# One ring tile of four PSUM banks in place of two two-bank tiles in the first phase of a ConvNeXt V2 block, with a new order of conv bursts and fewer channel-major quarters

## The chip, the cores and the metric

The kernel runs on one core of a Trainium2 chip. The time is the device time of one execution in microseconds (us), the median of several runs. All runs compared here were in the fast state. A ratio is the mean time of one kernel's fast runs over that of the other's from the same rounds, so it is not quite the ratio of the medians quoted beside it.

TensorE does the matmuls, ScalarE the activations out of PSUM, DVE (VectorE) the statistics and transposes, GpSimd (POOL in the profile) products in SBUF. The kernel uses PSUM as eight banks of 512 fp32 columns a partition: one, four and three in the pools below.

## The reference

```python
out = depthwise 3x3 convolution of x (1, 512, 512, 96)
h = layernorm(out, channels)
h = gelu(h @ w1)                                   # 96 -> 384
gx = sqrt(sum over all pixels of h*h + 1e-6)        # global, one value per channel
h = gamma * (h * gx / (mean(gx) + 1e-6)) + beta + h
return x + h @ w2                                   # 384 -> 96
```

The global sum splits the work into two phases. Phase 1 must see all pixels and make `sum h*h`. Phase 2 applies the result. The change touches phase 1 only.

## The kernel before

Phase 1 works on 128 blocks of four image rows (2048 pixels). In most of its *slots* TensorE makes the convolution of one block and the first MLP layer of an earlier block. The convolution is three *bursts* of 24 small matmuls on one accumulator of three banks (`psY`, one buffer), which ScalarE then copies out (`y_bf`, the *eviction*). The MLP is 12 banks of matmul output, each bank passed once through gelu by ScalarE.

The square sums come about in two ways. Output that stands channel-major (channels on partitions) goes through `bn_stats` on DVE, one instruction a bank. Output that stands pixel-major goes through *gram* matmuls on TensorE, three for each 128 pixels. A block has four quarters of 512 pixels, and `cm_quads` says how many are channel-major.

```python
def cm_quads(q):
    return 2 if is_res(q) else 3
...
psS = tile_pool(name="psS", bufs=1, PSUM)     # 1 bank: moments and gram sums, tile SG
psU = tile_pool(name="psU", bufs=2, PSUM)     # 2 x 2 banks: the MLP output
psY = tile_pool(name="psY", bufs=1, PSUM)     # 3 banks: the convolution
...
def pair(j):                                   # channels 128j.., two quarters, two banks
    U = psU.tile([128, 2, QW], f32, name="U")
    for t in range(2):
        cm_mm(U[:, t, :], j, t)
    act.activation(out=gsh[:, :, j, :], in_=U[:], func=Gelu_apprx_tanh)

def rest(n):                                   # two banks of the third quarter or of
    U = psU.tile([128, 2, QW], f32, name="U")  # pixel-major output
    ...
    act.activation(out=gms[b][:, c0:end], in_=Uf, func=Gelu_apprx_tanh)
...
# the order of a slot (cut)
conv(0); pair(0); conv(1); turn_x(s + 2)
pair(1); squares(0); gram_of_last(0)
pair(2); squares(1); gram_of_last(1)
rest(0); squares(2)
conv(2); evac()
rest(1); stats; rest(2); squares_rest()
```

`conv(n)` is burst n. Bursts 0 and 1 end in a drain of TensorE. No semaphore is written by hand: the recording layer (`tile.TileContext`) notes which instruction reads and writes which tile, and puts the waits in.

## Time and profile before

| | before |
|---|---|
| time | 1561.48 us (3 runs, 1561.41 to 1561.51) |
| conv evictions in 300 to 900 us | 80, so 7.5 us a slot |
| busy in that stretch: DVE, ScalarE, TensorE, GpSimd | 95, 93, 93, 89% |
| TensorE clock granted there | 1.00 |

The first fence is the busy table for 600 us in the middle of phase 1: length of the stretch, then for each engine busy us and instructions in brackets, then the granted TensorE clock, the share of the DMA engines, GB/s.

```profile
core 0: us, PE busy (x) PEld busy (x) DVE busy (x) ACT busy (x) POOL busy (x), PEclk, DMA share, GB/s
300.00:900.00 600.00, 557.30 (x9848) 269.83 (x9840) 572.30 (x963) 557.38 (x561) 537.04 (x403) 1.00 0.77 235
```

No engine is full. What sets the pace is seen in the timeline of one slot, first on TensorE (start, length, engine, operation, tiles, shapes, count, and in brackets the idle time before it and who ended it), then on ScalarE. All lines are of L32, a helper that records every operation, so the tile names tell them apart: Y is the convolution, U the MLP output, SG the statistics bank. The lengths of matmuls include their modelled ends and overlap; starts are what to compare.

```profile
531.53 0.88 PE L32 MATMUL Y<-xT,Wq 64*32 64x512 bf16 x24 [0.20 <-ACT y_bf L32]
532.53 0.60 PE L32 MATMUL U<-ynT,w1p 128*128 128x512 bf16 x2
533.06 0.86 PE L32 MATMUL Y<-xT,Wq 64*32 64x512 bf16 x24
534.05 0.60 PE L32 MATMUL U<-ynT,w1p 128*128 128x512 bf16 x2
...
538.94 0.87 PE L32 MATMUL Y<-xT,Wq 64*32 64x512 bf16 x24 [0.19 <-ACT y_bf L32]
```

```profile
533.22 1.02 ACT L32 ACTIVATE gsh<-U 128x1024 bf16<-128x1024 f32 x1
534.69 1.94 ACT L32 ACTIVATE gsh<-U 128x1024 bf16<-128x1024 f32 x2 [0.45 <-PE U L32]
536.51 1.03 ACT L32 ACTIVATE gm<-U 128x1024 bf16<-128x1024 f32 x1
537.42 1.47 ACT L32 ACTIVATE y_bf<-Y 128x1536 bf16<-128x1536 f32 x1
```

The first burst starts at 531.53 when the eviction is done. Pair, second burst and second pair follow; only then has ScalarE its second gelu (534.69, after 0.45 us of idleness). Three gelus and the eviction later, at 538.94, the next first burst can start. The waits of ScalarE in the 600 us say the same (total, times, longest):

```profile
ACT gsh L32 <- PE U L32: 42.4, 86, 1.5
```

### The profile page before, as it was taken

Reading aid. Unit: us, or ns where it says so; the run is one execution under the profiler, and the core shown is the slowest. Engines: PE = TensorE matmul, PEld = TensorE weight load, DVE = VectorE, ACT = ScalarE, POOL = GpSimd, SP = SyncE. Lnnn points to the kernel's source line nnn. Section 1 sums busy time; section 2 is a strip of 40 time slices with the busy share of each in tenths; the row PEclk is TensorE's granted clock in tenths of the full one; section 3 lists DMA queues with packets and bytes.
Section 4 is the critical chain, followed back from the end, with each engine's and each line's share of the span. In section 5 each row is a group of like instructions: output and inputs, shape, how many; then the busy total and the mean of one; then the engine's idle time right before and its main releaser. Section 6 shows DMA issues by size and latency. Waiting matters only on the chain. (4 is left out here: it accounts for less than half of the span.)

```text
span 1559.3 us, 54608 instructions
## 1 busy us (share of the span) xinstructions
PE 1438.9 (92%) x23119; PEld 819.7 (53%) x23119; DVE 1211.7 (78%) x2157; ACT 1436.7 (92%) x1306; POOL 1318.4 (85%) x933
## 2 busy tenths in 40 slices
PE   7889989999999999999999997789999999999998
PEld 3334444444444444444444443357777766676666
DVE  6749989999999999999999999955555555455555
ACT  3779989999999999999999999999999999899997
POOL 3459889989998998898899897459999999899997
PEclk8899999999999999999999999999999999999999
DMA  5568787777778778778868767879999999999996
GB/s 152 162 174 256 241 251 249 223 225 246 228 245 250 231 226 258 237 221 250 244 207 252 221 198 222 275 249 395 380 385 384 381 377 378 341 389 379 376 379 236
DMA packets 235467, 427.86 MB, mean 274 GB/s; under 512 B 34103, under 2 KB 148375, under 8 KB 235223
## 3 DMA queue, kind: packets, MB, share of 16 engines
q1 hardware_dynamic: 219972, 356.59, 70.4%
q0 software_dynamic: 13888, 67.64, 11.5%
q8 instruction: 181, 2.97, 0.8%
q14 instruction: 64, 0.52, 0.1%
q10 hardware_dynamic: 1362, 0.15, 0.1%
HBM read 272.78 MB, written 150.72 MB: 272 GB/s over the span
## 5 line engine op out<-in xcount | busy, mean ns | idle before, releaser
L32 PE MATMUL U<-ynT,w1p 128*128 128x512 bf16 x2292 | 664.4, 381 | 48.5 <-ACT gm L32 10.0
L32 ACT ACTIVATE gr<-U 128x1536 bf16<-128x1536 f32 (+1 forms) x384 | 519.1, 1456 | 13.1 <-PE U L32 11.3
L32 DVE BATCH_NORM_STATS2 bst<-gsh 128x6 f32<-128x512 bf16 x756 | 463.0, 674 | 21.7 <-ACT gsh L32 15.7
L32 DVE TENSOR_TENSOR o_sb<-O,xb 128x384 bf16<-128x384 f32 x512 | 277.9, 556 | 250.7 <-PE O L32 153.0
L32 POOL TENSOR_TENSOR yn<-y_bf,rbc 128x1536 bf16<-128x1536 bf16 x128 | 397.4, 3107 | 87.3 <-ACT rbc L32 31.0
L32 ACT ACTIVATE gsh<-U 128x1024 bf16<-128x1024 f32 x378 | 374.5, 1025 | 61.5 <-PE U L32 61.4
L278 POOL TENSOR_TENSOR xb<-xr,B2c 128x1536 f32<-128x1536 bf16 x126 | 394.8, 3135 | 33.9 <-DVE B2c L32 30.9
L32 ACT ACTIVATE gm<-U 128x1024 bf16<-128x1024 f32 x384 | 381.8, 1047 | 0.2
L32 PE MATMUL Y<-xT,Wq 64*32 64x511 bf16 (+1 forms) x8694 | 324.6, 391 | 32.9 <-ACT y_bf L32 25.8
L32 POOL TENSOR_TENSOR ysq<-y_bf 128x1536 bf16<-128x1536 bf16 x114 | 313.2, 2748 | 32.9 <-ACT y_bf L32 32.4
L32 PEld LDWEIGHTS <-w1p 128*128 128x128 bf16 x2292 | 181.6, 97 | 289.5 <-issue 203.3
L32 PEld LDWEIGHTS <-gr 128*128 128x128 bf16 x4584 | 236.8, 98 | 107.5 <-issue 23.4
L32 PE MATMUL O<-W2s,gr 128*128 128x96 bf16 x4584 | 257.2, 206 | 12.4 <-DVE o_sb L32 11.9
L32 DVE BATCH_NORM_STATS2 bst<-gm 128x6 f32<-128x512 bf16 x378 | 242.3, 679 | 29.7 <-ACT gm L32 29.7
L32 PEld LDWEIGHTS <-Wq 64*32 64x32 bf16 x9216 | 114.0, 91 | 212.5 <-issue 174.1
L32 ACT ACTIVATE y_bf<-Y 128x1536 bf16<-128x1536 f32 x121 | 177.5, 1467 | 16.2 <-PE Y L32 16.1
L32 DVE STREAM_TRANSPOSE xT<-xin 128x576 f32<-128x576 f32 (+1 forms) x256 | 180.4, 745 | 2.1 <-DMA xin<-in_x_dram 2.0
L32 PEld LDWEIGHTS <-gm 128*128 128x128 bf16 x1560 | 106.8, 98 | 66.3 <-issue 11.7
L32 PE MATMUL SG<-gm 128*128 128x128 bf16 x1560 | 126.1, 219 | 8.9 <-DVE SG L32 8.2
L32 PE MATMUL U<-w1p,ynT 128*128 128x384 bf16 (+2 forms) x780 | 126.5, 272 | 5.0 <-ACT gm L32 3.8
L250 POOL DMA_DIRECT2D xr<-in_x_dram x123 | 68.4, 556 | 35.9 <-POOL xb L278 35.9
L32 PEld LDWEIGHTS <-ynT 128*128 128x128 bf16 x780 | 67.3, 97 | 35.3 <-issue 15.4
(103 smaller groups left out, 696.6 us busy)
## 6 DMA issues: line engine op xcount, KB each, us to landing
ynT<-yn_dram SPq DMA_DIRECT2D x254, 384.0 KB
xin<-in_x_dram SPq DMA_DIRECT2D x126, 432.0 KB
yn_dram<-yn SPq DMA_DIRECT2D x512, 96.0 KB
xr<-in_x_dram POOLq DMA_DIRECT2D x128, 384.0 KB, 6.5
out_dram<-o_sb SPq DMA_DIRECT2D x127, 384.0 KB
g_dram<-gsh SPq DMA_DIRECT2D x126, 384.0 KB
gl<-g_dram SPq DMA_DIRECT2D x84, 384.0 KB
gl<-g_dram POOLq DMA_DIRECT2D x42, 384.0 KB, 7.2
```

The costliest lines, as they stand in the source:

```text
L32: r = f(*a, **k)
L250: pq.dma_start(out=xr[:], in_=x[0, r0:r0 + GR].rearrange("r w c -> (r w) c").rearrange("(p g) c -> p g c", g=PXP))
L278: pq.tensor_tensor(out=xb[:], in0=grp[q]["xr"][:], in1=bias[:, None, :].to_broadcast([128, PXP, C]), op=ALU.add)
```

## The change

The intent: with two two-bank tiles only one unit of gelu work can stand ahead of the second burst. Four banks used as a ring, in units of one or two banks, would let three banks stand ahead of it and one bank just behind it. One drain goes. The second half of the gram matmuls moves behind the third burst. In a third of the blocks one quarter turns from channel-major to pixel-major, to take load from DVE.

```diff
     def cm_quads(q):
-        return 2 if is_res(q) else 3
+        return 3 if q % 3 and not is_res(q) else 2
...
-        psU = p1.enter_context(tc.tile_pool(name="psU", bufs=2, ...PSUM))
+        psU = p1.enter_context(tc.tile_pool(name="psU", bufs=1, ...PSUM))
+        NB = 4
+        ring = psU.tile([128, NB, W], f32, name="U")
+        next_bank = [0]
+
+        def banks(n):
+            k = next_bank[0] % NB
+            if k + n > NB:
+                k = 0
+            next_bank[0] = k + n
+            return ring[:, k:k + n, :]
...
-            def pair(j): ...
-            def rest(n): ...
+            def unit(bank, n):          # n = 1 or 2 of the block's 12 banks
+                U = banks(n)
+                ...
...
-                conv(0); pair(0); conv(1); ...            (slot as above)
+                    conv(0)
+                    unit(0, 2)
+                    unit(2, 1)
+                    squares(0)
+                    conv(1, False)                        # no drain
+                    ...
+                    unit(3, 1)
+                    unit(4, 2)
+                    squares(1)
+                    gram_of_last(0)
+                    unit(6, 2)
+                    squares(2)
+                    ...
+                    conv(2)
+                    evac()
+                    gram_of_last(1)
+                    unit(8, 2)
+                    unit(10, 1)
+                    unit(11, 1)
+                    squares_rest(); stats
```

## The prediction

> **What bounds it now.** The busy table by stretch shows phase 1 until about 1020 us; the change touches only it. From 109 to 938 us each slot runs the conv of one block and the MLP of another. The ScalarE groups of 300 to 900 us hold 80 conv evictions: 7.49 us a slot, 111 slots. No engine is full there: DVE 95%, ScalarE 93%, TensorE 93%, GpSimd 89%. The timeline shows a ring. Between 531.53 and 538.94 us: first conv burst and drain 0.99 us, first pair 0.53, second burst and drain 0.99, second pair until its gelu starts 0.64, three gelus 0.91 each, eviction 1.47, which frees the only conv accumulator for the next first burst: 7.40 together, the period seen slot after slot. ScalarE idles 0.44 us in each, waiting for the second pair behind the second burst (waits: 42.4 us in these 600), since two two-bank tiles hold only one unit of lead. Other waits make it 7.49.
>
> **What changes.**
> - Three banks of gelu work, not two, stand ahead of the second burst, and a one-bank tile just behind it. ScalarE then has 0.91 + 0.48 us to cover a burst, which without its drain takes 0.81 us (the third burst's pace) instead of 0.99. The 0.44 us hole and the ring should go.
> - Two gelus of 1024 become four of 512. Back-to-back gelus start 0.91 us apart, and 0.93 just after an eviction; 1024 elements at the 0.833 ns that the Trainium skill's "ScalarE: Activation LUTs" (The pipeline for one element) measures are 0.853 us, so a split costs about 0.06 us; the "Perfetto Trace Analysis" page (Optimizing Scalar/DVE Operations) says about 51 ns for PSUM, which this trace supports. ScalarE: +0.12 us a slot, a floor of 4 x 0.91 + 4 x 0.48 + 1.33 = 6.9 us.
> - A third of the blocks lose three statistics of 0.61 us (DVE 7.14 to about 6.5 us a slot on average, still about 7.1 in the other blocks) and gain twelve gram matmuls at 0.055 us plus small pieces: TensorE +0.7 us in that third. From starts without waits, TensorE needs about 6.45 us in light slots, 7.15 in heavy.
> - Unchanged: GpSimd. Two products a slot take 5.78 us start to start, the variance chain 4.5 us per four slots: 6.9 us, plus about 0.27 us of DMA waits a slot now.
>
> **On the critical path.** The hole and the drain leave it; the split gelus enter. ScalarE and GpSimd then both stand near 6.9 us and nothing has slack, so GpSimd's DMA waits and SG waits become visible: I expect 7.12 us a slot. 0.37 x 111 = 41 us less, little elsewhere.
>
> **Predicted: 1521 us**, 8 in 10 between 1503 and 1547. Faster by over 2%: 0.66; within 2%: 0.31; slower: 0.03.
>
> **Right if** the conv evictions stand 7.0 to 7.2 us apart; the ScalarE wait for the second pair falls from 42 us to under 10; ScalarE and GpSimd rise to 96% or more of that stretch; DVE falls to about 92%; phase 2 is unchanged, and the end of phase 1 comes about 40 us earlier.
>
> **Wrong if** DVE, at 7.1 us in two of three blocks, delays the reset of the statistics bank and so TensorE, a wait that then grows with DVE; if GpSimd falls behind and its late normalised rows stall the MLP (slots then at 7.3 us or more, gain under 20 us); if heavy slots cost TensorE more than 0.7 us, because small matmuls do not hide their weight loads; or if the ring's wrap makes a two-bank tile wait for a late gelu.

(The 0.833 ns an element are in the subsection "Step-by-step: what each stage is for" of the page that the prediction names.)

## The result, and the profile after

| | before | after |
|---|---|---|
| time, median | 1561.45 us (4 runs) | 2497.01 us (4 runs, 2485.53 to 2498.66) |
| ratio | | 1.598 (1.593 to 1.603) |
| evictions from `psY` in 300 to 900 us | 80 | 41 (14.6 us a slot) |
| busy there: DVE, ScalarE, TensorE, GpSimd | 95, 93, 93, 89% | 46, 53, 69, 45% |
| TensorE clock over the run | 0.991 | 0.781 |

The results are right; the kernel is 60% slower. Every engine is idle more than before:

```profile
300.00:900.00 600.00, 415.51 (x5263) 179.89 (x5261) 274.97 (x444) 317.30 (x367) 272.74 (x202) 0.74 0.39 123
```

The clock row of the page (40 equal slices of the run, tenths of full speed) stands between 5 and 8 in phase 1 and at 9 again in phase 2. Before, all but the first two slices read 9.

```profile
PEclk8877777776767767677676766777555899999999
```

One slot of the changed kernel, nearly all of it at full clock (0.94 granted on average; it falls at the end), TensorE and then ScalarE:

```profile
501.92 0.88 PE L32 MATMUL Y<-xT,Wq 64*32 64x512 bf16 x24
502.91 0.60 PE L32 MATMUL U<-ynT,w1p 128*128 128x512 bf16 x2
504.68 0.38 PE L32 MATMUL U<-ynT,w1p 128*128 128x512 bf16 x1 [1.16 <-ACT gsh L32]
504.98 0.86 PE L32 MATMUL Y<-xT,Wq 64*32 64x512 bf16 x24
505.78 0.39 PE L32 MATMUL U<-ynT,w1p 128*128 128x512 bf16 x1
506.85 0.59 PE L32 MATMUL U<-ynT,w1p 128*128 128x512 bf16 x2 [0.68 <-ACT gsh L32]
...
508.56 0.59 PE L32 MATMUL U<-ynT,w1p 128*128 128x512 bf16 x2 [0.78 <-ACT gsh L32]
...
512.57 0.38 PE L32 MATMUL U<-w1p,ynT 128*128 128x256 bf16 x2 [1.66 <-ACT gm L32]
513.63 0.59 PE L32 MATMUL U<-w1p,ynT 128*128 128x128 bf16 x2 [0.68 <-ACT gm L32]
...
514.77 1.48 PE L32 MATMUL Y<-xT,Wq 64*32 64x512 bf16 x24
```

```profile
503.60 1.02 ACT L32 ACTIVATE gsh<-U 128x1024 bf16<-128x1024 f32 x1 [1.56 <-PE U L32]
505.09 0.60 ACT L32 ACTIVATE gsh<-U 128x512 bf16<-128x512 f32 x1 [0.47 <-PE U L32]
506.20 0.60 ACT L32 ACTIVATE gsh<-U 128x512 bf16<-128x512 f32 x1 [0.52 <-PE U L32]
507.48 1.02 ACT L32 ACTIVATE gsh<-U 128x1024 bf16<-128x1024 f32 x1 [0.68 <-PE U L32]
...
511.48 1.03 ACT L32 ACTIVATE gm<-U 128x1024 bf16<-128x1024 f32 x1
512.98 0.60 ACT L32 ACTIVATE gm<-U 128x512 bf16<-128x512 f32 x1 [0.47 <-PE U L32]
514.25 0.60 ACT L32 ACTIVATE gm<-U 128x512 bf16<-128x512 f32 x1 [0.67 <-PE U L32]
```

Read the two together. The first unit, two banks, is written at 502.91, its gelu runs 503.60 to 504.62, and the matmul of the next unit, which by the code goes to another bank, starts at 504.68. Its gelu starts at 505.09. So it goes on: 506.85 after the gelu that began at 506.20, 508.56 after the one of 507.48, 512.57 after the one of 511.48, 513.63 after the one of 512.98. Matmuls and gelus take turns. In the waits of 600 us there is now a line that was not there before, TensorE waiting for gelus:

```profile
PE U L32 <- ACT gsh L32: 91.5, 108, 1.2
PE U L32 <- ACT gm L32: 88.5, 82, 1.7
```

ScalarE's waits for TensorE are its counterpart; the 42.4 us of before became

```profile
ACT gsh L32 <- PE U L32: 192.1, 160, 3.2
ACT gm L32 <- PE U L32: 80.1, 122, 1.2
```

The slot from 501.92 to 514.77 takes 12.85 us. The next ends at 530.86 in the same timeline (not printed) and takes 16.09: there a burst lasts 1.48 us in place of 0.88, and the clock granted in that stretch is 0.61. From eviction to eviction the slots soon repeat in threes: 12.64 us at clock 1.00 (from 541.88), 16.33 at 0.60, 15.42 at 0.65.

### The profile page after: what moved, and what is told of

Read it like the earlier page. It is cut to its first block, busy times and chain, and to the rows that moved or that the text cites. A ratio compares the mean times of both kernels' runs of the same rounds, so it can differ in the third digit from the quotient of the medians.

```text
span 2496.9 us, 55852 instructions
## 1 busy us (share of the span) xinstructions
PE 1860.3 (75%) x23749; PEld 961.7 (39%) x23749; DVE 1171.7 (47%) x2027; ACT 1537.7 (62%) x1534; POOL 1318.0 (53%) x933
## 4 chain that ended last, share of the span: by engine, by line
PE 57%; ACT 28%; POOL 6%; issue 3%; DMA 2%; DVE 1%; SPq 1%; ACTq 0%; POOLq 0%
PE U L32 31%; PE Y L32 13%; ACT gsh L32 12%; ACT gm L32 10%; PE O L32 7%; PE SG L32 6%; ACT y_bf L32 6%; POOL xb L289 5%; DMA yn_dram<-yn 2%; SPq L32 1%; DVE o_sb L32 1%; POOL gl L256 1%; DMA ynT<-yn_dram 0%; POOL xr L261 0%; POOL yn L32 0%
## 5 line engine op out<-in xcount | busy, mean ns | idle before, releaser
L32 PE MATMUL U<-ynT,w1p 128*128 128x512 bf16 x2166 | 774.3, 447 | 311.2 <-ACT gsh L32 262.4
L32 DVE BATCH_NORM_STATS2 bst<-gsh 128x6 f32<-128x512 bf16 x756 | 488.9, 680 | 780.3 <-ACT gsh L32 775.0
L32 ACT ACTIVATE gsh<-U 128x1024 bf16<-128x1024 f32 x492 | 406.3, 826 | 590.8 <-PE U L32 590.8
L32 ACT ACTIVATE gm<-U 128x1024 bf16<-128x1024 f32 x498 | 412.6, 829 | 269.6 <-PE U L32 269.2
L32 PE MATMUL Y<-xT,Wq 64*32 64x511 bf16 (+1 forms) x8694 | 434.6, 509 | 9.0 <-DVE B2bc_f L32 3.7
L32 PE MATMUL U<-w1p,ynT 128*128 128x384 bf16 (+2 forms) x1032 | 217.4, 318 | 292.0 <-ACT gm L32 265.6
L32 PEld LDWEIGHTS <-ynT 128*128 128x128 bf16 x1032 | 109.9, 112 | 391.8 <-issue 369.3
L32 DVE BATCH_NORM_STATS2 bst<-gm 128x6 f32<-128x512 bf16 x252 | 166.4, 688 | 142.3 <-ACT gm L32 142.3
L32 PEld LDWEIGHTS <-gm 128*128 128x128 bf16 x2064 | 182.7, 126 | 124.4 <-issue 116.5
L32 PE MATMUL SG<-gm 128*128 128x128 bf16 x2064 | 218.7, 272 | 0.0
```

The source lines that it names most:

```text
L32: r = f(*a, **k)
```

## The experiments

**Theory "one tile".** To the layer that puts the waits in, the ring is one tile. A matmul that writes bank 2 of it waits for the gelu that reads banks 0 and 1 of it, since that is a read of the same tile. The waits in the built program agree: each wait names a counter and the value that it must have reached, and the value in front of a unit's first matmul is the count of the gelu of the unit just before, whatever its bank; in the kernel before it is the gelu two units back, the last reader of that buffer. Three rivals: the new order of bursts and units ("order"); the small units and the quarters, with their extra matmuls; and TensorE's clock, throttled for what it now does ("clock"). All outputs are right.

### split_tiles: the same change with separate tiles

```diff
-        ring = psU.tile([128, NB, W], f32, name="U")
+        def banks(n):        # psU: one buffer of two banks; psV: two buffers of one bank
+            if n == 2:
+                return psU.tile([128, 2, W], f32, name="U")[:]
+            return psV.tile([128, 1, W], f32, name="V")[:]
...
-                    unit(6, 2)
+                    unit(6, 1)
+                    unit(7, 1)
```

(The last slots of phase 1, which have no bursts, and two small users of the ring were fitted in the same way.)

> The changed kernel with its four banks held in separate tiles: one tile of two banks and two of one bank, used in turn A, B, C, A, B, C, A, B, C (so the two-bank unit of banks 6 and 7 becomes two of one bank); order, bursts and quarters as in the change. Theory 'one tile' (the ring is a single tile, and a unit's matmuls wait for the gelu of the unit just before it, whatever its bank): the waits go, slots of 7.0 to 7.3 us, 1505 to 1540 us, mean clock back to 0.98 or more. Rival 'order' (the new order of bursts and units stalls by itself) and rival 'clock' (TensorE is throttled by what it now does): still above 2000 us, clock still near 0.8.

Measured: 1553.32 us (6 runs), ratio 0.995 (0.993 to 0.997), clock 0.99. The loss of 936 us is gone, with order, small units (but for banks 6 and 7, now two units), missing drain and quarters all kept. Theory "one tile" stands and the rivals fall as causes of the loss. The hole is gone too: ScalarE's wait for the second pair, 42.4 us before, is no longer in its list. But the time is over the expected 1505 to 1540 us: even as intended, the change brings 0.5%. Two things hold it back. First, TensorE's timeline shows a heavy slot (24 gram matmuls and not 12) from its first burst at 534.60 to the next first burst, and the light slot that follows:

```profile
534.60 0.89 PE L32 MATMUL Y<-xT,Wq 64*32 64x512 bf16 x24
...
536.02 0.38 PE L32 MATMUL V<-ynT,w1p 128*128 128x512 bf16 x1
536.33 0.87 PE L32 MATMUL Y<-xT,Wq 64*32 64x512 bf16 x24
...
538.46 0.59 PE L32 MATMUL V<-ynT,w1p 128*128 128x512 bf16 x2
538.99 0.87 PE L32 MATMUL Y<-xT,Wq 64*32 64x512 bf16 x24
...
542.01 0.88 PE L32 MATMUL Y<-xT,Wq 64*32 64x512 bf16 x24
...
548.99 0.88 PE L32 MATMUL Y<-xT,Wq 64*32 64x512 bf16 x24 [0.15 <-ACT y_bf L32]
```

The heavy slot, 534.60 to 542.01, takes 7.41 us, with TensorE never waiting; the next takes 6.98. I had put the heavy slot at 7.15 us. The three switches a slot from full-array matmuls to the bursts' 64x32 tiling may be what I left out: the one-bank unit in front of a burst starts 0.31 us before it, where one bank otherwise takes 0.23 in this timeline, and two banks 0.53 against 0.43. The Trainium skill, "TensorEngine Tiling (Array Packing)", Key Properties, states that changing the tiling mode drains TensorE; these 0.1 us fit, and three of them are about what was missing, but no run here tests a switch by itself.

Second, and I had missed it: one heavy slot and two light ones average 7.12 us at this pace, just what was predicted, yet the 600 us hold 81 evictions, 7.4 us a slot. Seven slots of the 80 last 9.1 to 10.7 us. In each of them TensorE waits over 2 us for DVE to clear the statistics bank SG, and DVE comes to that only after three instructions that sum up `bn_stats`. The line of the waits, TensorE's wait in one such slot, and DVE just before it:

```profile
PE SG L32 <- DVE SG L32: 15.6, 7, 2.3
```

```profile
529.62 0.80 PE L32 MATMUL SG<-gm 128*128 128x128 bf16 x6 [2.26 <-DVE SG L32]
```

```profile
526.40 2.76 DVE L32 BATCH_NORM_AGGREGATE mv<-bst 128x2 f32<-128x192 f32 x3
```

The kernel before lost 7.3 us to this wait. Without the seven slots the mean is 7.18 us, so they cost about 0.22 us a slot, some 25 us in 111 slots (an estimate). The prediction had named this wait under "Wrong if".

### two_tiles: the ring as two tiles of two banks

```diff
-        ring = psU.tile([128, NB, W], f32, name="U")
+        rings = [psU.tile([128, 2, W], f32, name="U%d" % i) for i in range(2)]
...
-            return ring[:, k:k + n, :]
+            return rings[k // 2][:, k % 2:k % 2 + n, :]
```

> The changed kernel with its ring made of two tiles of two banks; nothing else differs, all units keep their size. Theory 'one tile': only neighbouring one-bank units, which share a tile, still wait for each other; some 0.4 us twice in a slot, so 7.5 to 8.2 us a slot and 1560 to 1640 us, clock above 0.95. Rivals 'order' and 'clock': above 2000 us.

Measured: 1910.51 us (4 runs), ratio 1.222, far over the expected 1560 to 1640 us, and clock 0.917, not above 0.95; 57 evictions in the 600 us, 10.5 us a slot. Only two pairs of one-bank units share a tile here, and still some 350 us are lost.

```profile
540.27 0.60 PE L32 MATMUL U<-w1p,ynT 128*128 128x384 bf16 x4
542.53 0.38 PE L32 MATMUL U<-w1p,ynT 128*128 128x128 bf16 x2 [1.67 <-ACT gm L32]
...
543.42 0.87 PE L32 MATMUL Y<-xT,Wq 64*32 64x512 bf16 x24
```

My 0.4 us a wait was right for the first pair of neighbours (0.43 to 0.62 us in this timeline) and wrong for the second. The gelu of bank 10 stands behind the eviction and a two-bank gelu in ScalarE's order, so the matmuls of bank 11 wait 1.67 us, and in TensorE's timeline the statistics and the next slot's first burst come only after them. One false wait costs as much as the queue ahead of what it waits for.

### ring_only: the ring tile alone, in the kernel before

```diff
-        psU = ...tile_pool(name="psU", bufs=2...)
+        psU = ...tile_pool(name="psU", bufs=1...)      # and the ring, as in the change
...
-                U = psU.tile([128, 2, QW], f32, name="U")
+                U = banks(2)
```

> The kernel before with nothing changed but its two two-bank tiles, which become the one ring tile of four banks; order, unit sizes, drains and quarters are the old ones. Theory 'one tile': every unit waits for the gelu before it, so six times about 1 us in the slot: 2000 to 2400 us, clock 0.75 to 0.85. Rivals 'order' and 'small units and quarters': within 2% of the kernel before, 1561 us.

Measured: 2113.01 us (4 runs), ratio 1.354, clock 0.91. One tile in place of two, and nothing else, costs 552 us; TensorE waits 93.9 and 86.7 us of the 600 for gelus, lines that the kernel before does not have. The clock fell less than I expected (0.75 to 0.85). "Order" and "small units and quarters" predicted 1561.

### ring_pairs: the changed kernel with six units a slot

```diff
-                    unit(2, 1)
+                    unit(2, 2)
...
-                    unit(3, 1)
...
-                    unit(10, 1)
-                    unit(11, 1)
+                    unit(10, 2)
```

> The changed kernel, one ring tile and all, with its four one-bank units in each slot joined into two of two banks (banks 2 and 3 before the second burst, 10 and 11 at the end), so six units a slot in place of eight. Theory 'one tile': the loss goes with the number of units, since each waits for the gelu before it; two handshakes less of about 1.1 us at full clock and 1.5 at the low one, in 111 slots, so 240 to 330 us less than 2497: 2130 to 2290 us. If the waits were tied to the banks and not to the number of units, 2400 us or more.

Measured: 2221.29 us (4 runs), ratio 1.424, clock 0.853, in the expected range. Eight turns a slot cost 276 us more than these six, though not by turns alone: the six of `ring_only` cost 108 us less again. Slots in which the granted clock is 1.00 take 10.88 us in `ring_only` (505.45 to 516.33), 11.29 here (495.03 to 506.32) and 12.64 in the changed kernel, so some 150 of the 276 us are there without any loss of clock (an estimate, 1.35 us in 111 slots). So the one-bank units, which were to give ScalarE its work sooner, made things worse while every unit was a turn.

### filled: the clock

Each unit of the changed kernel is followed by matmuls with zero weights, added to the gram sums.

```diff
+            def fill(n):
+                for _ in range(2 * n):
+                    pe.matmul(SG[:, 2 * NS:], lhsT=zrow[:, :128], rhs=zrow[:, :NCH * 128],
+                              start=False, stop=True, skip_group_check=True)
```

> The changed kernel, ring and all, with work that changes no result put into TensorE's waits: after each unit, two matmuls of 384 columns a bank with zero weights, added to the gram sums (24 a slot, about 3.8 us at full clock). It tells what of the loss is the low clock (0.78 mean, about 0.74 in the middle of phase 1). Theory 'the clock falls because TensorE idles in the waits of the one tile': the clock rises to 0.95 or more and the time falls, though work was added, to 2150 to 2350 us; the rest of the loss is the waits themselves. Rival 'clock' (TensorE is throttled for its load): the clock stays at 0.78 or below and the time rises above 2500 us.

Measured: 2367.35 us (4 runs), ratio 1.518, clock 0.99. The time is 17 us over the expected range, and the sign is clear: with some 3.9 us of work more a slot (an estimate: 24 matmuls, of which four take 0.65 us in its timeline, 502.06 to 502.71) TensorE runs at full clock and the kernel is 130 us faster. Rival "clock" said over 2500.

```profile
300.00:900.00 600.00, 499.90 (x6523) 257.40 (x6520) 290.00 (x473) 338.35 (x390) 289.07 (x218) 0.99 0.41 128
```

So the low clock comes with the waits, and costs at least 130 of the 936 us. The filler hides some: a slot of `filled` takes 13.87 us, one of the changed kernel at full clock 12.64. Had all its slots that pace and not the 14.80 of the repeating three, 111 of them would save some 240 us (an estimate). How much idleness lowers the clock these runs do not tell: `ring_only` keeps TensorE busy 69% of the 600 us like the changed kernel, with clock 0.93 there and not 0.74. The last slots of phase 1, which are units and no bursts, show one turn by itself in the changed kernel:

```profile
1924.88 1.02 ACT L32 ACTIVATE resg<-U 128x1024 bf16<-128x1024 f32 x1 [1.10 <-PE U L32]
1927.02 1.02 ACT L32 ACTIVATE resg<-U 128x1024 bf16<-128x1024 f32 x1 [1.11 <-PE U L32]
...
1951.86 1.02 ACT L32 ACTIVATE gr<-U 128x1024 bf16<-128x1024 f32 x1 [0.68 <-PE U L32]
1953.56 1.02 ACT L32 ACTIVATE gr<-U 128x1024 bf16<-128x1024 f32 x1 [0.68 <-PE U L32]
```

At the low clock (0.50 granted from 1916 to 1926) gelus stand 2.1 us apart, near the full clock (0.95 from 1950.2 to 1954) 1.7, of which 1.02 are the gelu and 0.68 the wait for the matmuls. In these slots of the kernel before, rows of gelus stand 0.91 to 0.92 us apart, back to back.

### quads_only and split_oldq: the quarters

```diff
# quads_only: the kernel before with
-        return 2 if is_res(q) else 3
+        return 3 if q % 3 and not is_res(q) else 2
# split_oldq: split_tiles with that line turned back
```

> The kernel before with nothing changed but a third of the blocks with two channel-major quarters. Theory 'one tile' says nothing of it beyond: the period of 7.40 us is a ring of TensorE and ScalarE that DVE is not in, so DVE falls from 95% to about 88% of the stretch and the time stays within 1%: 1550 to 1575 us. Rival 'quarters' (the twelve more gram matmuls and small pieces in a third of the slots make the loss): above 1700 us.

> The kernel with separate tiles (1553 us) with three channel-major quarters in all blocks again. There every third slot was bound by TensorE at 7.41 us, with 24 gram matmuls, and the others by ScalarE at about 6.98. If the quarters were what kept it at 1553: the heavy slots go, DVE stands at 7.1 to 7.2 us a slot, slots of 7.15 to 7.3 us, 1530 to 1550 us. If DVE was the limit that the quarters lifted: 7.4 us or more and 1555 us or more, with DVE above 97%.

Measured: `quads_only` 1582.40 us (4 runs), ratio 1.014; `split_oldq` 1536.18 us (4 runs), ratio 0.985. DVE fell to 86% in the first, as expected, and the time rose by 21 us, against an expectation of no change. The quarters cost 17 us with separate tiles as well. In the timeline of `quads_only` a slot with 24 gram matmuls runs 7.83 us from first burst to first burst (551.31 to 559.14), a light one 7.40 (534.87 to 542.27): half of the added matmuls stand ahead of the third pair and half ahead of the next unit, and ScalarE, which waits for both, starts the gelu of the latter 2.26 us after that of the second pair and not 1.83; DVE, which they relieve, was not in that ring. In a third of 111 slots 0.43 us are 16 us. `split_oldq`, in its expected range, is 1.5% faster than the kernel before, with ScalarE and DVE both at 97% in the 600 us. Its slots are of about 7.03 us, but it has the waits for SG as well (15.6 us), and its mean is 7.27.

### one_drain: testing the reading of the kernel before

```diff
-                conv(1)
+                conv(1, False)
```

> The kernel before with nothing changed but the drain after the second burst taken out (the change takes the same one out; the first one must stay, without it the race check refuses the kernel). My reading of the kernel before is a ring of 7.40 us through TensorE and ScalarE, and this drain costs it 0.99 - 0.81 = 0.18 us. If the ring is right: slots of 7.25 to 7.35 us against 7.49, 1540 to 1552 us. If DVE at 95% is the real limit: within 0.3% of the kernel before, 1557 to 1566 us.

Measured: 1544.61 us (4 runs), ratio 0.990 (0.988 to 0.991), 82 evictions in 600 us, 7.3 us a slot. DVE, at 95%, was not the limit; a drain of 0.18 us in the ring was worth 17 us. That is most of what `split_oldq`, which leaves out the same drain, gained in the same rounds: three banks ahead of the second burst and all else brought only 8 us more (1544.61 against 1536.18).

### pairs_first, pairs_first_q6 and split_q6: looking for a better version

```diff
# pairs_first: the kernel before with the second pair ahead of the second burst
                 conv(0)
                 pair(0)
+                if taps:
+                    pair(1)
                 conv(1)
...
-                pair(1)
+                if not taps:
+                    pair(1)
# pairs_first_q6, split_q6: pairs_first and split_tiles with
+        return 3 if q % 6 and not is_res(q) else 2
```

> The kernel before, its two two-bank tiles and its drains, with only the second pair moved ahead of the second burst: the lead that the change wanted from its ring, without a ring. My reading: the ring of 7.40 us (burst, pair, burst, pair, three gelus, eviction) loses its second burst and becomes burst, pair, four gelus, eviction: 0.99 + 0.64 + 4 x 0.91 + 1.47 = 6.74 us, below DVE's 7.14 us; the slot falls to 7.15 to 7.35 us, 1525 to 1547 us, and ScalarE's wait for the second pair, 42 us in 600, falls below 15. If the old tiles give no lead (the second pair waits for the last gelu of the slot before), 1555 us or more.

> As pairs_first, and every sixth block with two channel-major quarters, to take load from DVE (three statistics of 0.61 us in one block of six, 0.3 us a slot) for twelve gram matmuls in that block. If DVE at about 7.14 us a slot is then the limit: 5 to 15 us faster than pairs_first. If heavy slots cost more than DVE gains: 2 to 10 us slower.

> The kernel with separate tiles with the quarters taken in every sixth block: between every third (1553 us) and none (1536 us). If heavy slots cost in proportion, 1540 to 1548 us; if DVE at 97% with none was a limit as well, 1528 to 1536 us.

Measured: `pairs_first` 1583.77 us (4 runs), ratio 1.015: a miss. `pairs_first_q6` 1591.90 us (5 runs), ratio 1.020. `split_q6` 1532.99 us (6 runs, 1529.62 to 1545.07), ratio 0.984 (0.981 to 0.987), not to be told from `split_oldq`; its runs spread over both ranges that were expected, so whether DVE was a limit as well stays open. ScalarE's timeline of `pairs_first` shows its miss:

```profile
538.10 1.46 ACT L32 ACTIVATE y_bf<-Y 128x1536 bf16<-128x1536 f32 x1
...
541.28 1.94 ACT L32 ACTIVATE gsh<-U 128x1024 bf16<-128x1024 f32 x2
543.93 1.02 ACT L32 ACTIVATE gsh<-U 128x1024 bf16<-128x1024 f32 x1 [0.70 <-PE U L32]
544.85 1.02 ACT L32 ACTIVATE gm<-U 128x1024 bf16<-128x1024 f32 x1
545.75 1.46 ACT L32 ACTIVATE y_bf<-Y 128x1536 bf16<-128x1536 f32 x1
```

The hole of 0.44 us did not close. It moved one gelu on and became 0.70: now the third pair stands behind the second burst. The ring is burst, pair, a wait of 0.25 us for the last gelu of the slot before, pair, burst, six gram matmuls, third pair, two gelus, eviction, and its period is 7.65 us (538.10 to 545.75). I had counted the ring as if only the moved pair were in it. With two tiles of two banks there is no place for a unit right behind the burst. This is what separate one-bank tiles are good for.

## Why the prediction was wrong

The step that failed is "Three banks of gelu work, not two, stand ahead of the second burst, and a one-bank tile just behind it." Only one bank did: the gelu of the first two was over at 504.62, before the third was written at 504.68. Each unit's matmuls waited until the gelu of the unit before was done, as the turns in the timeline, `ring_only` (2113 us) and `split_tiles` (1553 us) show. All that was built on the step (no hole, a floor of 6.9 us, 7.12 us a slot, 41 us saved) spoke of another kernel.

- **The bound before** was read rightly: a ring of TensorE and ScalarE, no full engine. `one_drain` confirms it within its range.
- **The warning signs were at hand.** The changed kernel asks for one tile once and hands out slices of it; the old one asks for a fresh tile each time. I had seen in the built program that each unit waits for ScalarE, and took it for the wait of the bank's last reader without looking at which value it waits for (from memory). The Trainium skill, "Perfetto Trace Analysis", Identifying Dependency Chains, says to look at the semaphores that an instruction waits on; their values decide. Of waits for gelus, my list of what could go wrong had only the ring's wrap, one late wait in place of eight.
- **The clock** was not in the prediction. The Trainium skill, "TensorE: Matmul & The Clock Gate", section "A second HAM failure mode: psum-queue depth-cycling", tells that short idle times between groups of matmuls can make the clock fall and rise again. This trace agrees: 1.00, 0.60 and 0.65 in three slots that follow each other, and 0.99 in `filled`.
- **ScalarE's split gelus and the TensorE sum**, tested in `split_tiles`: two one-bank gelus take 0.95 us (537.20 to 538.15) against 0.91 for a pair, about as predicted; but heavy slots took 7.41 us and not 7.15, and the quarters cost 17 us where I had counted them as relief for DVE. GpSimd stood at 90%, not at the predicted 96 or more. With separate tiles and without the quarters, what is left of the idea is worth 26 us (`split_oldq`, against 1561.90 us in its rounds), not 41, and 17 of the 26 are the drain's.
- **DVE** lost load (88% in `split_tiles`, predicted about 92%), and it bought nothing, since DVE was not in the ring. Where DVE did hold TensorE, at the clearing of SG, the wait was 15.6 us with the quarters and 15.6 without.
- **Phase 2** was unchanged, as predicted: from the first of its long row of 1536-column gelus to the end it takes 530.9 us before (1028.44 to 1559.3) and 530.4 after (1966.52 to 2496.9).

What stays open: how the low clock and the turns share the 936 us exactly (at least 130 us for the clock, by the estimate above some 240); how much idleness brings the clock down; and how the 108 us between `ring_only` and `ring_pairs` split between order, drain, quarters and clock.

## What to carry to other kernels

Independent memory is not independent to the layer that orders the engines: a buffer cut out of one large tile carries that tile's waits, so a ring must be made of tiles that the layer knows apart, and the values of the waits in the built program should be read before believing in any overlap. When two engines hand work to and fro, find the ring that has the period of the slot and count every member again after a move, since a hole that is pushed out of one place comes back at the next unit. Relief for an engine that is not in the ring buys nothing, and the work put elsewhere for it may land in the ring.

## What the Trainium skill lacked or had wrong

- Tracking by tile: none of the pages that I read says that waits put in by a recording layer may cover a whole tile of several banks. "PSUM — Partial Sum Buffer", Summary: rules for kernel authors, advises another bank for a read while a matmul runs, and guarding by bank; `split_tiles` (1553 us) agrees that separate banks can be used at once, `ring_only` (2113 us) shows that choosing another bank is not enough.
- "TensorE: Matmul & The Clock Gate", HAM oscillation, gives a rule of no idle gaps over about 3.4 us. Here the clock fell to 0.74 although TensorE's longest wait for a gelu in the 600 us was 1.7 us; the section after it, on short idle times, fits better, without a figure. TensorE was busy 69% at clock 0.74 here, but also 69% at 0.93 in `ring_only`, and 83% at 0.99 in `filled`.
- "TensorEngine Tiling (Array Packing)", Key Properties, gives no figure for a switch of the tiling mode; in `split_tiles` the unit in front of a burst takes about 0.1 us more than the same unit elsewhere, which may be the switch (no run tests it by itself).
